# Declaring the two banks of a two-bank PSUM tile independent of each other

## The chip, the core and the metric

The kernel runs on one core of one Trainium2 chip. The metric is the device time of one execution in microseconds. The engines are named as in the profile: PE is TensorE (matrix products), DVE is VectorE, ACT is ScalarE, POOL is GpSimd, SP is SyncE, which issues the DMAs. PSUM is the memory that TensorE writes its products to; it is divided into banks of 512 fp32 numbers per partition.

## The reference

For each of four batches the reference normalises the columns of `q` and `k`, forms a 256 by 256 score matrix, takes its softmax and multiplies `v` by it. The 24,320 rows that result go through a feed-forward layer with a rational activation, 256 to 2048 to 256:

```
qn = q / (norm(q, axis=1) + 1e-6);  kn = k / (norm(k, axis=1) + 1e-6)
s = kn.transpose(0, 2, 1) @ qn / tau        # one 256 x 256 matrix a batch
a = softmax(s)
x = (v @ a).reshape(24320, 256)             # v: (4, 6080, 256)
h = x @ w_in                                # 256 -> 2048
P = a0 + a1*h + a2*h**2 + a3*h**3
Q = 1 + |b0|*|h| + |b1|*h**2
out = (P / (Q + 1e-6)) @ w_out              # 2048 -> 256
```

## The kernel before, in words

**Tiling.** The softmax matrix and `w_in` are multiplied into one fused weight for each batch, so that the main work goes straight from `v` to `h`. The rows are taken in groups of 512 (the twelfth group of a batch has 448), 48 groups in all. The 2048 hidden columns are taken in pairs of two times 128 columns, eight pairs a group, 384 pairs in all. A pair's `h` is a PSUM tile *hx* of two banks, one for each 128 columns. There are three such tiles, six banks; the other two banks are *acc*, into which the group's output is summed.

**One pair** (function `pair`, line 744). The steps that matter here, in the order of their data:

- *mm1(0)* and *mm1(1)* (line 758) on TensorE: six matmuls each, the first six into the low bank of hx, the other six into the high bank.
- Passes over both banks at once, 128 x 1024 elements: ScalarE reads hx for absolute values or squares and for the slope (lines 783 to 804), VectorE forms *prod* in some pairs (line 785) and *num1* (805), and *num2* (807), which writes the numerator without its constant back into hx. The denominator is made in the SBUF tile d, and from it ScalarE makes an approximate reciprocal r, in two passes.
- Operations on one bank each, 128 x 512, once for i = 0 (low bank) and once for i = 1 (high bank), lines 830 to 859. In half of the pairs (kind "S"): GpSimd multiplies d by r, *quot* on VectorE (line 819) multiplies hx by r in place, and *last* (line 825) makes g from d and hx. In the other half (kind "R"): quot writes its result to the SBUF tile gh, GpSimd multiplies d by gh, *rest* on VectorE (line 822) makes d from hx and d, and GpSimd makes gl. So the last reader of a bank is *last* in one half of the pairs and *rest* in the other.
- The second product (line 771) on TensorE, from g, or from gh and gl, into acc.

**Other users of hx tiles.** The score products of the next batch go to the low bank alone (line 541 and following); the transposed exponentials (line 668) and the fused weights (line 681) go to the high bank alone; the transposed rows of `v` (line 718) use both banks.

**What sets the order.** The kernel doesn't issue its steps as they are written. Each step is handed to a planner (class `Planner`, line 113) with an engine, a cost, a key (a due time) and the buffers that it reads and writes. The planner simulates the five engines and gives out one order of steps for each; `order()` is at line 159. To the planner the two banks of an hx tile are two buffers, "hA" and "hB", with users of their own: mm1(0) of a new pair may be placed as soon as the old pair's last user of hA is through, although hB of the same tile is still in use, and mm1(1) later. Then the steps are issued in that order. The wrapper `InOrder` (line 54) pins every instruction behind the one before it on its engine, so an engine's order is the planner's.

**What sets the waits.** The waits between engines are not the planner's. The framework that the kernel is written in follows every access to a tile and puts a semaphore wait wherever it finds that one instruction depends on an earlier one of another engine. The hx tiles are allocated whole, two banks in one tile.

Of the kernel before, what the change touches and what calls it, by code (L numbers as in the profile page):

```python
# [20 lines left out]
LAG = {  # L21
    "first": (-23.943, 0.779, 16.152, -2.628, 12.275, -14.299, 0.849, 12.204),
    "second": (64.578, 55.323, 59.143, 56.607, 7.413, 49.338, 52.686, 69.362),
    "line": (11.809, -44.33, -0.798, -23.493, 7.232, -28.691, -20.654, -32.78),
    "prod": (-25.799, -25.066, -7.177, -0.027, 1.503, -30.754, -29.951, -14.021),
    "abs": (22.851, -16.828, -6.381, 4.349, 3.845, 0.375, -1.748, -5.521),
    "slope": (-2.413, -14.175, 23.292, -11.592, 10.064, 22.358, 14.327, 33.823),
    "num1": (102.929, 82.894, 81.158, 62.614, 64.142, 120.209, 89.073, 104.516),
    "num2": (-4.828, -66.826, -23.076, -34.364, -51.549, -56.374, -41.833, -65.959),
# [24 lines left out]
class InOrder:  # L54


    def __init__(self, tc, engine):
        self.tc, self.engine = tc, engine

    def __getattr__(self, name):  # L60
        op = getattr(self.engine, name)

        def issue(*args, **kwargs):
            ins = op(*args, **kwargs)  # L64
            self.tc.keep_in_program_order(ins)
            return ins

        return issue
# [40 lines left out]
def flat(bufs):  # L109
    return [x for b in bufs for x in (b.both if isinstance(b, Pair) else [b])]  # L110
# [162 lines left out]
def tile_channel_attention_rational_ffn(  # L273
# [12 lines left out]
    nc = tc.nc  # L286
# [22 lines left out]

    FRONT = 12  # L310

    pe = InOrder(tc, nc.tensor)
    dve = InOrder(tc, nc.vector)
    act = InOrder(tc, nc.scalar)
    pool = InOrder(tc, nc.gpsimd)
    sp = InOrder(tc, nc.sync)

    SLOTS = {"hA": 3, "hB": 3, "acc": 1, "d": 3, "uu": 4, "r": 3, "gh": 6, "gl": 4, "g": 4, "w": 9, "kq": 4, "sq": 2, "ssq": 1,
# [27 lines left out]
    def banks(view=None):  # L346


        def whole(slot):
            t = homes["hx"][slot].rearrange("p (a b) -> p a b", a=2)  # L350
            return t if view is None else view(t)

        return Pair(Buf("hA", whole), Buf("hB", whole))

    def bank(tag):
        return Buf(tag, lambda slot: homes["hx"][slot][:, 512 * (tag == "hB") :][:, :512])

    def step(eng, cost, key, fn, reads=(), writes=(), port=False, rank=None):
        new = [b for b in flat(writes) if b.tag is not None and not b.writers]

        def run():
            for b in new:
                b.tile = b.view(b.slot)
            fn()

        plan.add(eng, cost, key, run, reads, writes, port, rank)

# [126 lines left out]
    class Attn:  # L494
# [3 lines left out]
        def __init__(self, b, begin, pace, end, gate=()):  # L498
            self.b, self.gate, self.kq = b, gate, [None, None]
            self.ssq = None  # L500
            first = b == 0
            sps = bank("hA") if first else None
            self.sacc = None if first else buf("sacc", [P, 512], F32)
            self.front = FRONT if b == 1 else 0
            if self.front:
                sps = buf("acc", [P, 2 * GT], F32, "fronts")
            for i in range(2 * NG):
                if i < self.front:
                    at = both = TIME["front"] + i * TIME["front_pace"]
                else:  # L510
                    at, both = begin + i * pace, begin + (i if first else i + 1 - i % 2) * pace
                self.half(i, at, both, sps)
            self.scores = sps if first else self.sacc
            self.softmax(end)
# [229 lines left out]
    def pair(m, at, vparts, w, acc):  # L744
        G, p = divmod(m, NFP)
        pn = groups[G % NG][1]
        n = T * pn
        s = n / 512
        (vhi, vlo), (whi, wlo) = vparts, w
        hx = banks()  # L750
        d, r = buf("d", [P, 2, GT]), buf("r", [P, 2, GT])
# [27 lines left out]
        def cost(per, fixed):  # L779
            return per * s + fixed  # L780

        if kind[1] == "F":
            fn = lambda: act.activation(c(kk), c(hx), AF.Abs, scale=b1)
            step("ACT", cost(0.87, 0.25), at + LAG["first"][p], fn, [hx], [kk], rank=at + 1.0)
            fn = lambda: dve.scalar_tensor_tensor(c(d), c(kk), b0, c(hx), op0=ALU.add, op1=ALU.mult)
            step("DVE", cost(1.06, 0.22), at + LAG["prod"][p], fn, [kk, hx], [d], rank=at + 1.0)
            fn = lambda: act.activation(c(d), c(d), AF.Abs)
            step("ACT", cost(0.87, 0.17), at + LAG["abs"][p], fn, [d], [d])
        else:
            fn = lambda: act.activation(c(d), c(hx), AF.Square)  # L790
            step("ACT", cost(0.87, 0.16), at + LAG["first"][p], fn, [hx], [d], rank=at + 1.0)
            fn = lambda: act.activation(c(kk), c(hx), AF.Abs, scale=b0)
            step("ACT", cost(0.87, 0.25), at + LAG["second"][p], fn, [hx], [kk], rank=at + 1.0)
            if kind[1] == "A":
                fn = lambda: act.activation(c(d), c(d), AF.Identity, scale=b1, bias=ONE)
                step("ACT", cost(0.87, 0.27), at + LAG["line"][p], fn, [d], [d])
            else:
                fn = lambda: pool.tensor_scalar(c(d), c(d), b1, ONE, op0=ALU.mult, op1=ALU.add)
                step("POOL", cost(1.06, 0.07), at + LAG["line"][p], fn, [d], [d])
            fn = lambda: pool.tensor_tensor(c(d), c(d), c(kk), op=ALU.add)  # L800
            step("POOL", cost(2.32, 0.06), at + LAG["sum"][p], fn, [d, kk], [d])

        fn = lambda: act.activation(c(y), c(hx), AF.Identity, scale=a3, bias=a2)
        step("ACT", cost(0.87, 0.33), at + LAG["slope"][p], fn, [hx], [y], rank=at + 3.0)
        fn = lambda: dve.tensor_tensor(c(y), c(y), c(hx), op=ALU.mult)
        step("DVE", cost(1.06, 0.16), at + LAG["num1"][p], fn, [y, hx], [y])
        fn = lambda: dve.scalar_tensor_tensor(c(hx), c(y), a1, c(hx), op0=ALU.add, op1=ALU.mult)
# [3 lines left out]
        fn = lambda: act.activation(c(r), c(d), AF.Abs_reciprocal_sqrt, bias=more)  # L811
        step("ACT", cost(0.87, 0.2), at + LAG["root"][p], fn, [d], [r], rank=at + 6.0)
        if kind[1] == "F":
            fn = lambda: pool.tensor_scalar(c(d), c(d), ones[:, 0:1], ONE, op0=ALU.mult, op1=ALU.add)
            step("POOL", cost(1.06, 0.07), at + LAG["one"][p], fn, [d], [d])
        fn = lambda: act.activation(c(r), c(r), AF.Square)
        step("ACT", cost(0.87, 0.2), at + LAG["square"][p], fn, [r], [r])

        def quot(i, out):
            dve.scalar_tensor_tensor(out, hx[:, i, :n], a0, r[:, i, :n], op0=ALU.add, op1=ALU.mult)  # L820

        def rest(i, out):
            dve.scalar_tensor_tensor(out, hx[:, i, :n], a0, d[:, i, :n], op0=ALU.add, op1=ALU.subtract)

        def last(i, out):
            dve.scalar_tensor_tensor(
                out, d[:, i, :n], 2.0, hx[:, i, :n], op0=ALU.subtract, op1=ALU.mult, reverse0=True
            )

        for i in range(2):  # L830
            h, key = hx.both[i], at + 0.1 * i
            old = [acc] if p or i else []
            end = p == NFP - 1 and i == 1
            t = Buf()
            if kind[0] == "S":
                g = buf("g", [P, GT])
                fn = lambda i=i: pool.tensor_tensor(d[:, i, :n], d[:, i, :n], r[:, i, :n], op=ALU.mult)
                step("POOL", cost(1.16, 0.06), key + LAG["again"][p], fn, [d, r], [t])
                step("DVE", cost(0.53, 0.23), key + LAG["quot"][p], lambda i=i: quot(i, hx[:, i, :n]), [h, r], [h])
                step("DVE", cost(0.53, 0.16), key + LAG["last"][p], lambda i=i, g=g: last(i, g[:, :n]), [d, t, h], [g], rank=at + 10.0)  # L840
                fn = lambda i=i, g=g, end=end, old=old: mm2(i, (w_out_sb,), (g,), not old, end)
                step("PE", 1.72 * s, key + LAG["out"][p], fn, [g, w_out_ok[p], *old], [acc])
                continue
            ghi, glo = buf("gh", [P, GT], F32R), buf("gl", [P, GT], F32R)
            step("DVE", cost(0.53, 0.2), key + LAG["quot"][p], lambda i=i, g=ghi: quot(i, g[:, :n]), [h, r], [ghi], rank=at + 10.0)
            fn = lambda i=i, g=ghi: pool.tensor_tensor(d[:, i, :n], d[:, i, :n], g[:, :n].bitcast(F32), op=ALU.mult)
            step("POOL", cost(1.16, 0.06), key + LAG["again"][p], fn, [d, ghi], [t])
            if kind[2] == "D":
                step("DVE", cost(0.53, 0.23), key + LAG["rest"][p], lambda i=i: rest(i, hx[:, i, :n]), [h, d, t], [h])
                fn = lambda i=i, g=glo: dve.tensor_tensor(g[:, :n], hx[:, i, :n], r[:, i, :n], op=ALU.mult)  # L850
                step("DVE", cost(0.53, 0.16), key + LAG["last"][p], fn, [h, r], [glo], rank=at + 10.0)
            else:
                left = Buf()
                step("DVE", cost(0.53, 0.2), key + LAG["rest"][p], lambda i=i: rest(i, d[:, i, :n]), [h, d, t], [left])
                fn = lambda i=i, g=glo: pool.tensor_tensor(g[:, :n], d[:, i, :n], r[:, i, :n], op=ALU.mult)
                step("POOL", cost(1.16, 0.06), key + LAG["last_pool"][p], fn, [d, left, r], [glo], rank=at + 10.0)
            fn = lambda i=i, g=ghi, old=old: mm2(i, (w_out_hi, w_out_lo), (g, g), not old, False)
            step("PE", 0.92 * s, key + LAG["out"][p], fn, [ghi, w_out_ok[p], *old], [acc])
            fn = lambda i=i, g=glo, end=end: mm2(i, (w_out_hi,), (g,), False, end)
            step("PE", 0.46 * s, key + LAG["out_lo"][p], fn, [glo, w_out_ok[p], acc], [acc])  # L860
# [37 lines left out]
    for G in range(TG):  # L898
        b, g = divmod(G, NG)
        at = T0 + G * NFP * II  # L900
# [47 lines left out]
```

## Time and profile before

| | |
|---|---|
| median of 3 runs | 2874.55 us (2873.23 to 2874.65) |
| the profiled execution | 2872.88 us |
| its span, first to last instruction | 2871.1 us |
| TensorE matmuls busy | 2642.3 us (92% of the span) |
| VectorE busy | 2480.3 us (86%) |
| ScalarE busy | 2246.2 us (78%) |
| GpSimd busy | 2290.1 us (80%) |

How to read the profile: busy time is the union of an engine's instructions. In rows of operations, `hx<-vhi,w` means that the tile hx is written from vhi and w; buffer numbers are left out, and 128x512 is partitions by elements. All instructions carry line 64, that of the wrapper, so they are told apart by their tiles: `d<-hx,coef,d` is rest, `g<-d,hx` is last, `hx<-hx,coef,r` and `gh<-hx,coef,r` are quot, `hx<-uu,coef,hx` is num2, `hx<-vhi,w` and `hx<-vlo,w` are mm1. `PE hx L64 <- DVE d L64: 84.0, 96, 1.6` in the view of waits says that TensorE, before instructions that write hx, was idle for 84.0 us in 96 places, at most 1.6 us in one, until a VectorE instruction that writes d had ended.

### The profile page before, as it was taken

Reading aid. Unit: us, or ns where it says so; the run is one execution under the profiler, and the core shown is the slowest. Engines: PE = TensorE matmul, PEld = TensorE weight load, DVE = VectorE, ACT = ScalarE, POOL = GpSimd, SP = SyncE. Lnnn points to the kernel's source line nnn. Section 1 sums busy time; section 2 is a strip of 40 time slices with the busy share of each in tenths; the row PEclk is TensorE's granted clock in tenths of the full one; section 3 lists DMA queues with packets and bytes.
Section 4 is the critical chain, followed back from the end, with each engine's and each line's share of the span. In section 5 each row is a group of like instructions: output and inputs, shape, how many; then the busy total and the mean of one; then the engine's idle time right before and its main releaser. Section 6 shows DMA issues by size and latency. Waiting matters only on the chain.

```text
span 2871.1 us, 30342 instructions
## 1 busy us (share of the span) xinstructions
PE 2642.3 (92%) x10304; PEld 1858.2 (65%) x10304; DVE 2480.3 (86%) x2911; ACT 2246.2 (78%) x2285; POOL 2290.1 (80%) x1725
## 2 busy tenths in 40 slices
PE   7899999999998999999999999999999999999998
PEld 6666667666665666666676666666677666666666
DVE  8888898898978989987788998898788898898897
ACT  5777787687778878877778888787787888788886
POOL 6697788787768878878977888788896788787786
PEclk9999999999999999999999999999999999999999
DMA  8300002000100000002210000001220000000000
GB/s 306 125 15 15 30 8 79 15 15 29 41 18 15 23 22 15 22 29 81 74 57 14 30 15 15 30 15 45 73 72 23 22 15 15 30 15 15 29 8 14
DMA packets 69324, 109.97 MB, mean 38 GB/s; under 512 B 5296, under 2 KB 53936, under 8 KB 69168
## 3 DMA queue, kind: packets, MB, share of 16 engines
q1 hardware_dynamic: 69168, 108.03, 11.2%
q8 instruction: 81, 1.33, 0.2%
q14 instruction: 75, 0.61, 0.1%
HBM read 83.10 MB, written 24.90 MB: 38 GB/s over the span
## 4 chain that ended last, share of the span: by engine, by line
PE 48%; DVE 33%; issue 6%; POOL 6%; ACT 5%; DMA 0%; DVEq 0%; SPq 0%; POOLq 0%; ACTq 0%
PE hx L64 31%; PE acc L64 17%; DVE hx L64 12%; DVE d L64 7%; DVE uu L64 6%; DVE g L64 5%; POOL d L64 4%; DVE gh L64 3%; ACT uu L64 2%; ACT r L64 1%; ACT d L64 1%; POOL gl L64 1%; POOL ssq L64 1%; POOL orow L64 1%; ACT sq L64 0%
## 5 line engine op out<-in xcount | busy, mean ns | idle before, releaser
L64 PE MATMUL hx<-vhi,w 128*128 128x512 f32 (+1 forms) x3072 | 1097.3, 411 | 181.7 <-DVE d L64 77.8
L64 PEld LDWEIGHTS hx<-vhi,w 128*128 128x128 f32 x3072 | 578.5, 188 | 450.3 <-DVE d L64 136.5
L64 POOL TENSOR_TENSOR d<-d,gh 128x512 f32<-128x512 f32 (+1 forms) x384 | 484.1, 1281 | 267.4 <-DVE gh L64 266.9
L64 PE MATMUL acc<-g,w_out_sb 128*128 128x512 f32 (+1 forms) x1536 | 688.9, 587 | 1.1 <-DVE g L64 1.1
L64 ACT ACTIVATE uu<-hx,babs 128x1024 f32<-128x1024 f32 (+1 forms) x384 | 423.8, 1104 | 276.7 <-PE hx L64 276.7
L64 PE MATMUL hx<-vlo,w 128*128 128x512 f32 (+1 forms) x1536 | 600.5, 391 | 0.0
L64 POOL TENSOR_TENSOR gl<-d,r 128x512 fp32r<-128x512 f32 (+1 forms) x384 | 489.3, 1281 | 74.5 <-DVE d L64 70.9
L64 POOL TENSOR_TENSOR d<-d,r 128x512 f32<-128x512 f32 (+1 forms) x384 | 480.8, 1273 | 39.4 <-ACT r L64 36.5
L64 DVE SCALAR_TENSOR_TENSOR hx<-uu,coef,hx 128x1024 f32<-128x1024 f32 (+1 forms) x384 | 488.8, 1273 | 3.5
L64 DVE TENSOR_TENSOR uu<-uu,hx 128x1024 f32<-128x1024 f32 (+1 forms) x384 | 461.5, 1202 | 29.9 <-ACT uu L64 29.9
L64 PEld LDWEIGHTS acc<-g,w_out_sb 128*128 128x128 f32 x1536 | 289.9, 189 | 273.2 <-issue 254.9
L64 ACT ACTIVATE uu<-hx,coef 128x1024 f32<-128x1024 f32 (+1 forms) x384 | 457.3, 1191 | 0.0
L64 ACT ACTIVATE d<-d 128x1024 f32<-128x1024 f32 (+1 forms) x288 | 301.0, 1045 | 170.6 <-DVE d L64 165.6
L64 ACT ACTIVATE r<-d 128x1024 f32<-128x1024 f32 (+1 forms) x384 | 401.6, 1047 | 39.9 <-POOL d L64 37.0
L64 ACT ACTIVATE r<-r 128x1024 f32<-128x1024 f32 (+1 forms) x384 | 402.1, 1048 | 5.8
L64 DVE SCALAR_TENSOR_TENSOR d<-uu,babs,hx 128x1024 f32<-128x1024 f32 (+1 forms) x288 | 364.1, 1264 | 45.8 <-ACT uu L64 42.3
L64 POOL TENSOR_SCALAR d<-d,ones 128x1024 f32<-128x1024 f32 (+1 forms) x288 | 321.9, 1118 | 86.3 <-ACT r L64 86.1
L64 DVE SCALAR_TENSOR_TENSOR d<-hx,coef,d 128x512 f32<-128x512 f32 (+1 forms) x384 | 282.7, 741 | 123.8 <-PE hx L64 79.5
L64 DVE SCALAR_TENSOR_TENSOR g<-d,hx 128x512 f32<-128x512 f32 (+1 forms) x384 | 256.9, 679 | 99.8 <-PE hx L64 78.4
L64 PEld LDWEIGHTS hx<-vlo,w 128*128 128x128 f32 x1536 | 290.1, 189 | 58.5 <-issue 13.8
L64 DVE SCALAR_TENSOR_TENSOR hx<-hx,coef,r 128x512 f32<-128x512 f32 (+1 forms) x384 | 288.2, 751 | 22.6 <-ACT r L64 12.9
L64 DVE SCALAR_TENSOR_TENSOR gh<-hx,coef,r 128x512 fp32r<-128x512 f32 (+1 forms) x384 | 269.3, 740 | 25.3 <-ACT r L64 15.0
(101 smaller groups left out, 2982.5 us busy)
## 6 DMA issues: line engine op xcount, KB each, us to landing
vst<-in_v_dram SPq DMA_DIRECT2D x44, 512.0 KB, 3.4
out_dram<-orow SPq DMA_DIRECT2D x44, 512.0 KB, 2.6
kq<-in_k_dram SPq DMA_DIRECT2D x78, 256.0 KB, 3.4
kq<-in_q_dram SPq DMA_DIRECT2D x78, 256.0 KB, 3.7
d<-in_moe_w_in_dram SPq DMA_DIRECT2D x8, 512.0 KB, 6.5
r<-in_k_dram SPq DMA_DIRECT2D x10, 256.0 KB, 6.0
r<-in_q_dram SPq DMA_DIRECT2D x10, 256.0 KB, 6.0
d<-in_moe_w_out_dram SPq DMA_DIRECT2D x4, 512.0 KB, 5.6
```

The costliest lines, as they stand in the source:

```text
L64: ins = op(*args, **kwargs)
```

## The change

The steps, their instructions and the order stay. Each step that uses a single bank of an hx tile, and is either a step of TensorE or one of those marked `lone` (quot, rest and last of a pair), now notes which slot and bank it uses while its instructions are issued. For every instruction of such a step, the new function `apart` goes through the last 40 noted instructions on the other bank of the same tile and tells the framework, for those of another engine, that the two don't depend on each other. Steps over both banks and steps of ScalarE note nothing; neither do VectorE's steps for the score sums and the fused weights.

```
     half = [None]
     seen = {}

     def apart(eng, ins):
         if half[0] is None:
             return
         slot, bank = half[0]
         for other, old in seen.get((slot, 1 - bank), ()):
             if other is not eng:
                 tc.declare_no_dep(ins.ins, old.ins, reason="the two use different banks of one tile")
         mine = seen.setdefault((slot, bank), [])
         mine.append((eng, ins))
         del mine[:-40]
```

`InOrder` calls it after each instruction, and `step` sets the note:

```
-    def step(eng, cost, key, fn, reads=(), writes=(), port=False, rank=None):
+    def step(eng, cost, key, fn, reads=(), writes=(), port=False, rank=None, lone=False):
         new = [b for b in flat(writes) if b.tag is not None and not b.writers]
+        own = {id(b): b for b in (*flat(reads), *flat(writes)) if b.tag in ("hA", "hB")}
 
         def run():
             for b in new:
                 b.tile = b.view(b.slot)
+            used = {(b.slot, b.tag == "hB") for b in own.values()}
+            half[0] = used.pop() if len(used) == 1 and (eng == "PE" or lone) else None
             fn()
+            half[0] = None
...
-                step("DVE", cost(0.53, 0.23), key + LAG["quot"][p], lambda i=i: quot(i, hx[:, i, :n]), [h, r], [h])
+                step("DVE", cost(0.53, 0.23), key + LAG["quot"][p], lambda i=i: quot(i, hx[:, i, :n]), [h, r], [h], lone=True)
```

The other steps of quot, rest and last get `lone=True` in the same way.

More of the change, by code (lines that the diff above doesn't have):

```diff
@@ L54, with __init__ @@
 class InOrder:
-    def __init__(self, tc, engine):
-        self.tc, self.engine = tc, engine
+    def __init__(self, tc, engine, log=None):
+        self.tc, self.engine, self.log = tc, engine, log
     def __getattr__(self, name):
@@ L65, in issue @@
             self.tc.keep_in_program_order(ins)
+            if self.log is not None:
+                self.log(self, ins)
             return ins
@@ L310, in tile_channel_attention_rational_ffn @@
     FRONT = 12
[L312 to L315, printed above, removed]
+    half = [None]
+    seen = {}
+    def apart(eng, ins):
+        if half[0] is None:
+            return
+        slot, bank = half[0]
[5 more added lines that the diff above has]
+        del mine[:-40]
+    pe = InOrder(tc, nc.tensor, apart)
+    dve = InOrder(tc, nc.vector, apart)
+    act = InOrder(tc, nc.scalar, apart)
+    pool = InOrder(tc, nc.gpsimd, apart)
     sp = InOrder(tc, nc.sync)
@@ L838, in pair @@
                 step("POOL", cost(1.16, 0.06), key + LAG["again"][p], fn, [d, r], [t])
-                step("DVE", cost(0.53, 0.23), key + LAG["quot"][p], lambda i=i: quot(i, hx[:, i, :n]), [h, r], [h])
-                step("DVE", cost(0.53, 0.16), key + LAG["last"][p], lambda i=i, g=g: last(i, g[:, :n]), [d, t, h], [g], rank=at + 10.0)
+                step("DVE", cost(0.53, 0.23), key + LAG["quot"][p], lambda i=i: quot(i, hx[:, i, :n]), [h, r], [h], lone=True)
+                step("DVE", cost(0.53, 0.16), key + LAG["last"][p], lambda i=i, g=g: last(i, g[:, :n]), [d, t, h], [g], rank=at + 10.0, lone=True)
                 fn = lambda i=i, g=g, end=end, old=old: mm2(i, (w_out_sb,), (g,), not old, end)
@@ L844, in pair @@
             ghi, glo = buf("gh", [P, GT], F32R), buf("gl", [P, GT], F32R)
-            step("DVE", cost(0.53, 0.2), key + LAG["quot"][p], lambda i=i, g=ghi: quot(i, g[:, :n]), [h, r], [ghi], rank=at + 10.0)
+            step("DVE", cost(0.53, 0.2), key + LAG["quot"][p], lambda i=i, g=ghi: quot(i, g[:, :n]), [h, r], [ghi], rank=at + 10.0, lone=True)
             fn = lambda i=i, g=ghi: pool.tensor_tensor(d[:, i, :n], d[:, i, :n], g[:, :n].bitcast(F32), op=ALU.mult)
@@ L848, in pair @@
             if kind[2] == "D":
-                step("DVE", cost(0.53, 0.23), key + LAG["rest"][p], lambda i=i: rest(i, hx[:, i, :n]), [h, d, t], [h])
+                step("DVE", cost(0.53, 0.23), key + LAG["rest"][p], lambda i=i: rest(i, hx[:, i, :n]), [h, d, t], [h], lone=True)
                 fn = lambda i=i, g=glo: dve.tensor_tensor(g[:, :n], hx[:, i, :n], r[:, i, :n], op=ALU.mult)
-                step("DVE", cost(0.53, 0.16), key + LAG["last"][p], fn, [h, r], [glo], rank=at + 10.0)
+                step("DVE", cost(0.53, 0.16), key + LAG["last"][p], fn, [h, r], [glo], rank=at + 10.0, lone=True)
             else:
                 left = Buf()
-                step("DVE", cost(0.53, 0.2), key + LAG["rest"][p], lambda i=i: rest(i, d[:, i, :n]), [h, d, t], [left])
+                step("DVE", cost(0.53, 0.2), key + LAG["rest"][p], lambda i=i: rest(i, d[:, i, :n]), [h, d, t], [left], lone=True)
                 fn = lambda i=i, g=glo: pool.tensor_tensor(g[:, :n], d[:, i, :n], r[:, i, :n], op=ALU.mult)
```

## The prediction

> **What bounds the kernel now.** I read the page first (busy times, clock, chain), then the windows, then the waits of TensorE and of VectorE from 100 us on, then a timeline of a few microseconds. The page's first part, its clock row and its chain:
>
> ```profile
> span 2871.1 us, 30342 instructions
> ...
> PE 2642.3 (92%) x10304; PEld 1858.2 (65%) x10304; DVE 2480.3 (86%) x2911; ACT 2246.2 (78%) x2285; POOL 2290.1 (80%) x1725
> ...
> PEclk9999999999999999999999999999999999999999
> ...
> PE 48%; DVE 33%; issue 6%; POOL 6%; ACT 5%; DMA 0%; DVEq 0%; SPq 0%; POOLq 0%; ACTq 0%
> ```
>
> No engine is full. TensorE comes nearest, at a clock of 0.9 or more all through, and the chain that ended last passes between TensorE (48%) and VectorE (33%): the two wait for each other. The windows give the stretch between the preparation of the weights and the last group:
>
> ```profile
> core 0: us, PE busy (x) PEld busy (x) DVE busy (x) ACT busy (x) POOL busy (x), PEclk, DMA share, GB/s
> 100.00:2850.00 2750.00, 2552.68 (x9945) 1786.84 (x9945) 2386.99 (x2766) 2184.57 (x2205) 2225.95 (x1689) 1.00 0.09 30
> ```
>
> Of these 2750 us TensorE is idle for 2750.0 - 2552.7 = 197.3 and VectorE for 2750.0 - 2387.0 = 363.0. DMA has a share of 0.09 and bounds nothing. The waits say what ended that idle time (total, times, longest):
>
> ```profile
> PE hx L64 <- DVE d L64: 84.0, 96, 1.6
> PE hx L64 <- DVE g L64: 74.4, 89, 3.7
> PE hx L64 <- DVE hx L64: 17.1, 36, 1.7
> ...
> DVE d L64 <- PE hx L64: 79.5, 67, 4.2
> DVE g L64 <- PE hx L64: 78.4, 71, 1.8
> DVE d L64 <- ACT uu L64: 42.3, 52, 3.2
> DVE d L64 <- POOL d L64: 37.9, 41, 2.7
> DVE uu L64 <- ACT uu L64: 29.9, 18, 3.6
> DVE gh L64 <- ACT r L64: 15.0, 8, 3.2
> DVE hx L64 <- ACT r L64: 12.9, 31, 0.9
> ```
>
> TensorE waited 84.0 + 74.4 + 17.1 = 175.5 us, 89% of its 197.3, for VectorE before a matmul into an hx tile. VectorE waited 79.5 + 78.4 = 157.9 us, in 67 + 71 = 138 stalls, for TensorE's matmuls into hx. The second sum is the odd one. The VectorE operations that stall there are *rest* (d<-hx,coef,d) and *last* (g<-d,hx). What they read in hx was rewritten by VectorE itself in *num2*, a whole pass after the pair's own matmuls; their other input comes from GpSimd. No matmul makes any data for them. The wait can only be for matmuls of the next pair, which have begun in the other bank of the same tile. The timeline shows one such knot (start, length, idle before and who ended it):
>
> ```profile
> 1731.37 1.14 POOL L64 TENSOR_SCALAR d<-d,babs 128x1024 f32<-128x1024 f32 x1
> 1731.60 0.68 DVE L64 SCALAR_TENSOR_TENSOR g<-d,hx 128x512 f32<-128x512 f32 x1
> ...
> 1732.22 0.62 PE L64 MATMUL acc<-gh,w_out_lo 128*128 128x512 f32 x2
> 1732.32 0.76 DVE L64 SCALAR_TENSOR_TENSOR hx<-hx,coef,r 128x512 f32<-128x512 f32 x1
> ...
> 1733.13 0.50 PE L64 MATMUL hx<-vhi,w 128*128 128x512 f32 x1 [0.29 <-DVE hx L64]
> ...
> 1734.42 0.39 PE L64 MATMUL hx<-vhi,w 128*128 128x512 f32 x1
> 1734.90 0.69 DVE L64 SCALAR_TENSOR_TENSOR g<-d,hx 128x512 f32<-128x512 f32 x1 [1.83 <-PE hx L64]
> ...
> 1735.65 0.50 PE L64 MATMUL hx<-vhi,w 128*128 128x512 f32 x1 [0.84 <-DVE g L64]
> ```
>
> *last* of the low bank ends at 1732.28 and frees it. TensorE is through with acc at 1732.84 and could begin the next pair there, but waits 0.29 us for *quot* on the high bank (hx<-hx,coef,r). Then *last* of the high bank, whose hx input is ready at 1733.08, waits 1.83 us until the sixth matmul into the low bank has ended. Because it is that late, TensorE's second block, into the high bank, waits 0.84 us; this wait is for a true use of the bank, but its length is the false wait's doing.
>
> **The change, part by part.** It adds no instruction and no wait and leaves each engine's order; the bookkeeping runs while the program is built. It takes out waits between TensorE steps that use one bank and VectorE's quot, rest and last, where the two use different banks of one tile.
>
> VectorE's false waits. By the argument above all 138 stalls of rest and last on TensorE fall away: 157.9 us of VectorE's time.
>
> TensorE's false waits. Those ended by quot (17.1 us) are all false, since last or rest on the same bank still follows and it is that which frees the bank. Those ended by rest and last (84.0 + 74.4) are of three sorts: false, as the first block's in the knot can be; true but made long by a stall of VectorE, as the 0.84 us; or true without one. The view doesn't part them. As 138 stalls of VectorE face 96 + 89 = 185 of these waits, most belong to the first two sorts. TensorE's side is therefore worth between 17.1 and 175.5 us. It can be worth a little more, because a record outlasts the pace:
>
> ```profile
> 1734.18 0.40 PE L64 MATMUL hx<-vlo,w 128*128 128x512 f32 x1
> ```
>
> It takes 0.40 us, but the next matmul starts 0.24 later (the row at 1734.42). So 0.16 us of each of the 96 + 89 + 36 = 221 stalls is counted as busy, an estimate of 35 us, and the ceiling is 175.5 + 35 = 210 us. The Trainium skill, "Perfetto Trace Analysis", Identifying the Most-Contended Engine, goes further: matmul busy time says little of the room left, and the weight loads' share is to be read. By that TensorE (65%) would have far more room than VectorE (86%), and a floor would be VectorE's 2480 us. The trace agrees with the first half, by the 0.16 us; for the second no run here shows room beyond the waits, and the sum does without it.
>
> How the two add up. They don't: in the knot the same 1.8 us stands in both ledgers. A microsecond is gained only if both engines gain it, so I take the smaller, VectorE's 157.9. From it goes what comes late next. When rest and last come early, VectorE meets its next operation's inputs from ScalarE and GpSimd early too, and its waits for these, 42.3 + 37.9 + 29.9 + 15.0 + 12.9 = 138.0 us now, grow. The trace doesn't show by how much. One bound is today's density, 138.0 us on 2387.0 of work, which makes 158 x 0.058 = 9 us; the other is all 157.9. I take 26, a sixth, nearer to the low end, because the nearest row is the knot: GpSimd is already at its next operation at 1731.37, so the input of the stalled *last* had lain ready about 3.5 us when it ran. The gain is 157.9 - 26 = 132 us.
>
> The other pairs that become independent (score products, transposes of the exponentials, fused weights, each in one bank) are costed at nothing: what they wait for is mostly the true owner of their bank, and waits on quot, rest and last stand in the rows above already.
>
> The profiled execution took 2872.9 us, 1.8 more than its span; the sum against it is 2872.9 - 132 = 2741 us. The median of the runs, 2874.55, lies 0.06% above it, which I neglect. About 0.2% (6 us) is what a measurement of this kernel can tell from no change.
>
> **The rivals.** (a) *The gain is handed back.* VectorE runs early into ScalarE and GpSimd, which are 78% and 80% busy and partly fed by TensorE, and waits there instead. For it: 138.0 us of such waits exist. Against: both engines have some 20% of slack, and GpSimd in the knot was ahead. If two thirds of 157.9 return, the gain is 53 us: 2820.
>
> (b) *The change doesn't do what it says.* Each instruction waits until an engine's count of finished work reaches a value. Where the operation truly needed stands behind the falsely needed one in that order, the wait stays the same. For it: the second block's wait in the knot is of that kind. Against: rest and last need nothing of TensorE at all, so there no other operation can keep the wait. If nothing moves: 2873.
>
> (c) *Slower.* While TensorE writes one bank, VectorE now reads and writes its neighbour in the same tile, which the old waits forbade. Should the 138 freed operations be held up by it, they would take longer. These are the rows (min/median/max, ns; the last is an operation of this size that was held up, in the preparation of the weights):
>
> ```profile
> L64 DVE SCALAR_TENSOR_TENSOR d<-hx,coef,d x384: 673/746/752, 117.2 to 2855.8; 128x512 f32<-128x512 f32 x176, 128x448 f32<-128x448 f32 x16
> L64 DVE SCALAR_TENSOR_TENSOR g<-d,hx x384: 609/683/690, 129.4 to 2861.0; 128x512 f32<-128x512 f32 x176, 128x448 f32<-128x448 f32 x16
> ...
> L64 DVE SCALAR_TENSOR_TENSOR d<-uu,d x6: 672/688/1895, 76.3 to 96.9; 128x512 uint32<-128x512 uint32 x4, 128x512 f32<-128x512 f32 x2
> ```
>
> The held-up one took 1.895 - 0.688 = 1.2 us more. At that price 138 operations cost 166 us against 157.9 gained: 2881 us. It decides from 157.9 / 138 = 1.14 us an operation. Against: with TensorE busy 92% of the time and writing other tiles, the slowest of 384 is 7 ns from the median. The Trainium skill, "PSUM — Partial Sum Buffer", PSUM bank collisions, puts the conflict at the single bank and says that accesses to different banks run clean; by that the price is nothing. The rows agree for banks of other tiles, and for the two banks of one tile no run here shows it yet.
>
> (d) *More than forecast:* the ceiling of TensorE's side, 210 us, with nothing returned: 2663.
>
> **How the numbers follow.** The forecast, a gain of 60 to 210 us, has 0.80. Handed back, 6 to 60 us, has 0.11. Nothing moves 0.05, slower 0.03, beyond the ceiling 0.01. The range runs from the ceiling, 2663, to about where two thirds are handed back, 2825. Faster by over 0.2% is 0.80 + 0.11 + 0.01 = 0.92; within it 0.05; slower 0.03.
>
> **What would show it.** In the profile after, "DVE d <- PE hx" and "DVE g <- PE hx" should nearly vanish and "PE hx <- DVE hx" with them; "PE hx <- DVE d" and "<- DVE g" should fall together from 158 to 60 or less. VectorE's waits for ScalarE and GpSimd should rise by some 26 us; if they rise by 100, it is rival (a). Counts and durations should stay: medians of 746 ns for rest and 683 for last; were they to grow by tenths of a microsecond, it is (c). TensorE's busy share of the span should rise to about 95%. The prediction is wrong if the time falls by less than 48 us, or if it falls while those rows of VectorE on TensorE stay.

## The result, and the profile after

The changed kernel takes 2692.7 us in the median (2692.11 to 2693.56, 4 runs), the kernel before 2874.18 beside it. The ratio is 0.937, with a 95% interval of 0.935 to 0.939: 181.5 us or 6.3% faster. The forecast was 2741 us, with a range of 2663 to 2825. The gain is larger than the 132 us that the sum gave.

The page of the changed kernel, the lines that answer to those of before:

```profile
span 2691.8 us, 30390 instructions
...
PE 2601.5 (97%) x10304; PEld 1864.0 (69%) x10304; DVE 2473.1 (92%) x2911; ACT 2238.9 (83%) x2285; POOL 2287.1 (85%) x1725
...
DVE 38%; PE 33%; POOL 11%; issue 8%; ACT 8%; DMA 1%; SPq 0%; DVEq 0%; POOLq 0%; ACTq 0%
```

Each engine executes as many operations as before. The 48 instructions more are of the kind that isn't counted as busy. The profiled span is 2871.1 - 2691.8 = 179.3 us shorter. TensorE's busy time became shorter by 2642.3 - 2601.5 = 40.8 us, VectorE's by 2480.3 - 2473.1 = 7.2. For each of the two the rest of the 179.3 is idle time that went. In the chain that ended last, TensorE's share fell from 48% to 33%; VectorE's rose from 33% to 38% and GpSimd's from 6% to 11%.

The waits of TensorE and VectorE from 100 us on (total, times, longest), in the order of the rows of before:

```profile
PE hx L64 <- DVE d L64: 6.3, 21, 1.6
PE hx L64 <- DVE g L64: 26.2, 24, 2.0
...
DVE d L64 <- ACT uu L64: 25.9, 23, 3.2
DVE d L64 <- POOL d L64: 54.0, 65, 2.8
DVE uu L64 <- ACT uu L64: 27.0, 19, 3.2
DVE gh L64 <- ACT r L64: 15.4, 10, 3.2
DVE hx L64 <- ACT r L64: 13.4, 28, 1.7
```

Three rows are gone altogether: VectorE's rest and last on TensorE (157.9 us before) and TensorE on quot (17.1). TensorE's other waits for VectorE at hx fell from 158.4 to 6.3 + 26.2 = 32.5 us. VectorE's waits for ScalarE and GpSimd were 138.0 us and are 25.9 + 54.0 + 27.0 + 15.4 + 13.4 = 135.7: in sum, what VectorE gained didn't come back there. The sum hides two movements: GpSimd's row rose by 54.0 - 37.9 = 16.1 us, and ScalarE's four fell from 100.1 to 81.7, by 18.4. The knot of the prediction, at the same pair, in the timeline of the changed kernel:

```profile
1628.11 0.69 DVE L64 SCALAR_TENSOR_TENSOR g<-d,hx 128x512 f32<-128x512 f32 x1
...
1628.83 0.76 DVE L64 SCALAR_TENSOR_TENSOR hx<-hx,coef,r 128x512 f32<-128x512 f32 x1
...
1629.19 0.39 PE L64 MATMUL hx<-vhi,w 128*128 128x512 f32 x1
...
1629.70 0.69 DVE L64 SCALAR_TENSOR_TENSOR g<-d,hx 128x512 f32<-128x512 f32 x1
...
1630.33 0.61 PE L64 MATMUL hx<-vhi,w 128*128 128x512 f32 x2
```

The first matmul into the low bank (1629.19) starts while quot works on the high bank (1628.83 to 1629.59), and *last* of the high bank starts at 1629.70, 0.11 us behind quot, while those matmuls run; before, it stood 1.83 us. The 0.61 us row at 1630.33 holds the sixth matmul into the low bank and the first into the high bank, one right behind the other: the 0.84 us of TensorE are gone too.

The operations themselves didn't become slower (min/median/max in ns, the rows that rival (c) hung on):

```profile
L64 DVE SCALAR_TENSOR_TENSOR d<-hx,coef,d x384: 671/747/754, 118.1 to 2676.5; 128x512 f32<-128x512 f32 x176, 128x448 f32<-128x448 f32 x16
L64 DVE SCALAR_TENSOR_TENSOR g<-d,hx x384: 610/682/691, 130.4 to 2681.7; 128x512 f32<-128x512 f32 x176, 128x448 f32<-128x448 f32 x16
```

### The profile page after: what moved, and what is told of

It is laid out like the page before. It is cut to its first block, busy times and chain, and to the rows that moved or that the text cites. A ratio compares the mean times of both kernels' runs of the same rounds, so it can differ in the third digit from the quotient of the medians.

```text
span 2691.8 us, 30390 instructions
## 1 busy us (share of the span) xinstructions
PE 2601.5 (97%) x10304; PEld 1864.0 (69%) x10304; DVE 2473.1 (92%) x2911; ACT 2238.9 (83%) x2285; POOL 2287.1 (85%) x1725
## 4 chain that ended last, share of the span: by engine, by line
DVE 38%; PE 33%; POOL 11%; issue 8%; ACT 8%; DMA 1%; SPq 0%; DVEq 0%; POOLq 0%; ACTq 0%
PE hx L64 18%; PE acc L64 15%; DVE hx L64 13%; DVE d L64 9%; DVE uu L64 7%; POOL d L64 7%; DVE g L64 4%; DVE gh L64 3%; ACT uu L64 3%; ACT r L64 2%; POOL gl L64 2%; POOL ssq L64 2%; DVE vlo L64 1%; ACT d L64 1%; POOL orow L64 1%
## 5 line engine op out<-in xcount | busy, mean ns | idle before, releaser
L64 DVE SCALAR_TENSOR_TENSOR d<-uu,babs,hx 128x1024 f32<-128x1024 f32 (+1 forms) x288 | 364.2, 1264 | 29.3 <-ACT uu L64 25.9
L64 DVE SCALAR_TENSOR_TENSOR hx<-hx,coef,r 128x512 f32<-128x512 f32 (+1 forms) x384 | 288.4, 751 | 22.7 <-ACT r L64 13.4
L64 DVE SCALAR_TENSOR_TENSOR gh<-hx,coef,r 128x512 fp32r<-128x512 f32 (+1 forms) x384 | 269.4, 740 | 23.9 <-ACT r L64 15.4
```

## The experiments

Theory A is that of the prediction: VectorE's false stall is the root of the knot, and TensorE's second block inherits its length. Rival B says that TensorE's side alone costs. Later runs ask what sets the end now, and whether more waits of this kind can go.

**One direction at a time.** `apart` declares only for instructions of one engine:

```
-            if other is not eng:
+            if other is not eng and eng is dve:      # the other run: eng is pe
```

> Half of the change: only VectorE's rest, last and quot are declared independent of earlier TensorE instructions on the other bank; TensorE still waits for VectorE's operations on the other bank. Theory A (the knot: VectorE's false stall is the root, and TensorE's second block only inherits its length) expects most of the gain here: VectorE's waits on TensorE at rest and last go from 157.9 us to under 5, TensorE's waits on VectorE at hx fall from 175.5 to 70-110 us, with quot's 17 still there, and the time is 2735 to 2785 us. Rival B (TensorE's own false waits are what costs, VectorE's stalls are slack): 2830 us or more.

Measured: 2718.0 us (ratio 0.946, 0.944 to 0.947), 156 us faster than before. The waits:

```profile
PE hx L64 <- DVE g L64: 41.2, 49, 1.5
PE hx L64 <- DVE d L64: 15.4, 42, 1.6
PE hx L64 <- DVE hx L64: 10.9, 36, 1.7
```

VectorE's false stalls are gone, and TensorE's waits at hx fell from 175.5 to 41.2 + 15.4 + 10.9 = 67.5 us, although nothing was declared for TensorE: 108 of the 175.5 were inherited. Even quot's false waits are shorter (10.9 us instead of 17.1). The gain is larger than A expected. VectorE's five rows for ScalarE and GpSimd, however, grew here, from 138.0 to 50.2 + 45.4 + 28.1 + 16.4 + 16.0 = 156.1 us. One of them, which was 42.3 us before and is 25.9 with the whole change:

```profile
DVE d L64 <- ACT uu L64: 45.4, 58, 3.2
```

> The other half: only TensorE's one-bank steps are declared independent of earlier VectorE operations on the other bank; VectorE's rest and last still wait for the next pair's matmuls. Theory A expects little: quot's 17.1 us vanish and some of TensorE's first-block waits, but VectorE's 157.9 us at rest and last stay above 130 and the second block still waits for them; time 2800 to 2857 us. Rival B expects most of the 181 us: 2735 us or less. If the two halves together give 181 us, they add; if they give less, each needs the other.

Measured: 2826.55 us (0.983, 0.981 to 0.985), 48 us faster. The knot stays:

```profile
DVE d L64 <- PE hx L64: 73.3, 60, 4.6
DVE g L64 <- PE hx L64: 51.9, 51, 1.6
```

VectorE still stalls 125.2 us, a little less than A expected, and at the same pair as above *last* waits 1.23 us for the sixth matmul. Rival B falls. The two directions give 156 + 48 = 204 us one by one and 181.5 together, so some 22 us stand in both. The figure is rough: three of the four executions of this run took 2825.6 to 2828.1 us at a granted clock of 0.989, the fourth 2816.4 at 0.994, and the kernel before ran at 0.992 or 0.993; by the fourth it would be 32 us. VectorE's five rows for ScalarE and GpSimd fell here, to 42.0 + 28.3 + 28.0 + 15.0 + 12.8 = 126.1 us; the row shown above fell by 14.0, more than the sum:

```profile
DVE d L64 <- ACT uu L64: 28.3, 19, 3.2
```

**Half of the pairs.** `lone=True` stays at quot and last of kind S only, or at quot and rest of kind R only.

> The change for half of the pairs: quot and last of kind S are declared, quot and rest of kind R are not. VectorE's stalls before the change were 78.4 us at last and 79.5 at rest. Theory A (the gain follows VectorE's ledger) expects half of the 181 us, 75 to 110: 2765 to 2800, with the row of last on TensorE under 3 us and that of rest at 60 to 95. Rival: a stall taken away here only comes back at the next knot of the other kind; the row of rest grows beyond 110 and the gain is under 50 us, 2825 or more.

Measured: 2778.51 us (0.967, 0.965 to 0.968), 96 us faster; rest waits 72.9 us for TensorE, last no longer.

> The other half: quot and rest of kind R are declared, quot and last of kind S are not. Theory A: 75 to 110 us again, 2765 to 2800, the row of rest on TensorE under 3 us and that of last at 60 to 95; the two halves together give about the whole. Rival: under 50 us, 2825 or more, with the row of last beyond 110.

Measured: 2785.0 us (0.969, 0.968 to 0.970), 89 us faster; last waits 79.0 us, rest no longer. Both as A expected. The halves give 185 us, the whole 181.5: a stall taken away at one kind of pair doesn't come back at the other.

**Without quot.** The two quot steps lose their `lone=True`:

```
-                step("DVE", ..., lambda i=i: quot(i, hx[:, i, :n]), [h, r], [h], lone=True)
+                step("DVE", ..., lambda i=i: quot(i, hx[:, i, :n]), [h, r], [h])
```

> The whole change except that quot is not declared. The prediction held the waits ended by quot (17.1 us of TensorE's idle time) to be false and part of the gain. Theory A expects that row to come back at 15 to 30 us and the time at 2705 to 2725 us. Rival: quot's waits are covered, because the block behind them would wait for last or rest soon after in any case; then the time stays within 6 us of the changed kernel's 2692.7.

Measured: 2698.76 us (0.939, 0.937 to 0.940). The row is back with 11.1 us in 36 places, but the time is only 6 us above the changed kernel's and the intervals of the ratios overlap. Neither expectation is met clearly: the false waits for quot are real and worth some 6 us at most.

**More than the change.** In `values`, the transposes note the bank of each half (`half[0] = (slot.low.slot, c)` ahead of the inner loop).

> The change and more: the transposes of the rows of v, a step over both banks, note the bank for each half of their instructions, so that the first four no longer wait for the other bank's last user. In the changed kernel's profile TensorE waits 6.3 us at hx for VectorE's d, most of it of this kind. Expected: that row goes to 2 us or less and the time falls by 0 to 6 us, 2687 to 2693; rival: the wait only moves to the fifth transpose, and nothing is gained.

Measured: 2693.13 us (0.937, 0.936 to 0.938), no difference; the row reads 6.2 us instead of 6.3. The rival holds: a wait for the same VectorE operations stays.

ScalarE's and VectorE's steps for the fused weights could not be declared in this way. They write the buffers w, which matmuls into the other bank read, and a declaration takes away every dependency between two instructions, also the one through w. This was left as it is, and no run tests it.

**What sets the end.** TensorE is at 97%, so its work was cut: the second product's matmuls with gl are not issued (`fn = lambda: None` for that step), an estimated 174 us of TensorE's pace.

> The changed kernel without the 768 matmuls acc<-gl,w_out_hi (the low part's second product is left out of the sum; its inputs are still made, and each engine's order is otherwise the same). It takes about 768 x 0.23 = 174 us of TensorE's pace away. Question: what sets the end now, TensorE (97% busy) or VectorE (92%) with its waits for ScalarE and GpSimd. Theory A (TensorE is now the bound in most places): the time falls by 90 us or more, to 2600 or less. Rival C (VectorE with its 136 us of waits for ScalarE and GpSimd is as near, 2473 + 136 + small gaps = about 2640): it falls by 60 us at most, to 2633 or more.

Measured: 2702.02 us (0.940, 0.939 to 0.942), 9 us *slower* than the changed kernel. Theory A of this run (TensorE is the bound) falls by far; the time is on rival C's side, but a rise was in neither. Page and waits:

```profile
PE 2495.2 (92%) x9536; PEld 1710.9 (63%) x9536; DVE 2472.3 (92%) x2911; ACT 2238.7 (83%) x2285; POOL 2286.2 (85%) x1725
```

```profile
PE hx L64 <- DVE g L64: 63.6, 64, 2.5
PE hx L64 <- DVE d L64: 59.2, 99, 1.8
```

TensorE merely waits more: 122.8 us at hx instead of 32.5. Why the time rises by 9 us is open. The granted clock is lower, 0.986 to 0.989 against 0.992 to 0.994, and within this run the time goes with it: 2705.5 us at 0.986, 2698.2 at 0.989, or 2.4 us for a thousandth. By this estimate the 5 thousandths are worth some 12 us, as much as the rise; no run tests it.

> The kernel before without the same 768 matmuls. Theory A (before, the knot of VectorE and TensorE set the end: VectorE stalls until six matmuls are through, whatever TensorE does elsewhere) expects little: 174 us less of TensorE's work give 20 to 70 us, 2805 to 2855, and VectorE's waits on TensorE at rest and last stay above 110 us. Rival B (TensorE's load set the end before, too): 120 us or more, 2755 or less.

Measured: 2871.01 us (0.999, 0.998 to 1.000), 3 us, even less than A expected here. TensorE's waits at hx rose from 175.5 to 133.9 + 118.4 + 26.4 = 278.7 us. The clock was lower here too, 0.981 to 0.984 against 0.991 to 0.993; by the same estimate that hides some 24 us, and the gain at an equal clock would be about 27, as A expected. Either way it is a small part of 174: TensorE's load was not the bound before either. So VectorE's work was cut instead. *num1* is done on the low bank only; its high bank is left out:

```
-        fn = lambda: dve.tensor_tensor(c(y), c(y), c(hx), op=ALU.mult)
+        fn = lambda: dve.tensor_tensor(y[:, 0, :n], y[:, 0, :n], hx[:, 0, :n], op=ALU.mult)
```

> The changed kernel with num1 done on the low bank only: the multiplication of the high bank's slope by h is left out, the number and order of instructions are the same. By the rows of the two widths (1202 ns for 128x1024, about 680 for a VectorE operation of 128x512) this takes 384 x 0.52 = 200 us off VectorE. The runs with less TensorE work gave nothing, which was against the expectation that TensorE is the bound. Theory D (VectorE with its waits for ScalarE and GpSimd sets the end): the time falls by 70 to 130 us, to 2560 to 2625, where TensorE, at a pace of about 2550 plus the start, becomes the next bound. Rival E (no engine sets the end alone; the fixed order with three hx tiles holds all of them): less than 40 us, 2653 or more.

Measured: 2656.28 us (0.924, 0.923 to 0.926). VectorE's busy time fell by 2473.1 - 2291.3 = 181.8 us, the time by 36. Rival E holds, though 36 is close to its limit of 40. VectorE's waits:

```profile
DVE d L64 <- POOL d L64: 91.4, 107, 3.6
DVE d L64 <- ACT uu L64: 76.4, 94, 3.2
DVE hx L64 <- ACT r L64: 36.3, 51, 2.5
DVE uu L64 <- ACT uu L64: 32.2, 32, 3.2
DVE gh L64 <- ACT r L64: 20.7, 16, 3.7
```

These five sum to 257.0 us, 121.3 more than in the changed kernel: here the freed time is handed back to ScalarE and GpSimd, the very thing that didn't happen with the change.

> The changed kernel with both cuts: num1 on the low bank only and without the 768 matmuls of the low part's second product. If TensorE is the next bound behind VectorE (theory D), taking 174 us of it now counts: at least 40 us below the run with less VectorE work alone. Rival E: within 15 us of that run.

Measured: 2642.32 us (0.920, 0.918 to 0.921), 14 us below the run with less VectorE work alone. Rival E again.

> The kernel before with num1 on the low bank only, again 200 us less for VectorE. Theory D with the knot on VectorE's own path: VectorE was the bound before too, only with 158 us of false stalls in its ledger; the time falls by 90 to 180 us, to 2695 to 2785, and the false stalls stay above 110 us. Rival E (the knot of the two engines sets the pace, whoever has less work): less than 50 us, 2825 or more.

Measured: 2822.41 us (0.982, 0.980 to 0.984), 51 us faster than before, far from D's 90 and just beyond E's 50. The false stalls grew from 157.9 to 101.4 + 99.3 = 200.7 us, and the five rows for ScalarE and GpSimd from 138.0 to 65.1 + 54.2 + 32.4 + 28.1 + 19.3 = 199.1: with less work VectorE comes earlier, to the knot and to the other engines, and stands there.

**VectorE's waits for itself.** The condition in `apart` becomes `if other is not eng or eng is dve`, together with the transposes by bank:

> A candidate beyond the change: the transposes of the rows of v note the bank of each half (no gain on their own), and VectorE's instructions are declared independent of VectorE's own earlier ones on the other bank. Where quot on the high bank follows quot on the low bank, a wait for its own engine costs 0.04 us (the start of 1732.32 after an end of 1732.28) to 0.11 us; the program has 72 such waits fewer. Theory D: the few that go are VectorE's time, a gain of 3 to 8 us, 2685 to 2690. Rival: the waits move to the next instruction, no difference.

Measured: 2669.21 us (0.929, 0.927 to 0.930), 23 us faster than the changed kernel, with intervals apart; it beats both kernels. The gain is larger than expected, and of another kind. The same pair as above:

```profile
1613.85 0.68 DVE L64 SCALAR_TENSOR_TENSOR g<-d,hx 128x512 f32<-128x512 f32 x1
...
1614.44 0.75 DVE L64 SCALAR_TENSOR_TENSOR hx<-hx,coef,r 128x512 f32<-128x512 f32 x1
```

Quot starts 0.59 us after *last*, before that has ended (1614.53); in the changed kernel it starts 0.72 after. VectorE's busy time is 2450.4 us, 22.7 less, because operations overlap; its idle time is the same (2668.5 - 2450.4 = 218.1 against 218.7). My count of 72 waits was the wrong one. In the program, 272 waits for the instruction just before, on the other bank, became 2, most of the others turning into waits for an older instruction, which is done by then: 22.7 / 272 = 0.08 us each.

## Why the prediction was right, point by point

*False waits of VectorE, 157.9 us, all fall away.* Right: both rows are gone, and the run with VectorE's direction alone shows that they were the root. *It adds no instruction and no wait* was not quite right: there are 48 instructions more, none of them counted as busy.

*TensorE's waits are partly inherited.* Right: 108 of 175.5 us went when only VectorE's direction was declared. The records' overhang was estimated at 35 us; TensorE's busy time fell by 40.8.

*"They don't add", so the smaller ledger.* The two ledgers do overlap, by some 22 us between the two directions. But as a cap the smaller one was undersized. TensorE's side lost 175.5 - 32.5 = 143.0 us of waits and 40.8 of overhang, 183.8 in all. VectorE's side lost 157.9 us of stalls, 2.3 at the five rows, 7.2 of busy time and, to make up the span's 179.3, 11.9 in smaller rows and gaps that I had not counted.

*26 us come back as waits for ScalarE and GpSimd.* This is the mis-sized term: it measured -2.3 us. As the price of VectorE alone coming early it was near: with VectorE's direction alone the five rows grew by 18.1 us, and GpSimd's row grew by 16.1 with the whole change. The step that failed is that ScalarE was taken to stay where it is: its four rows fell by 18.4. ScalarE had itself been waiting for TensorE's matmuls into hx. Its largest wait, in the kernel before and in the changed kernel:

```profile
ACT uu L64 <- PE hx L64: 276.7, 188, 6.2
```

```profile
ACT uu L64 <- PE hx L64: 163.1, 124, 6.2
```

With VectorE's direction alone this wait is 205.4 us, with TensorE's alone 226.7. It is TensorE's direction that lowers VectorE's waits for ScalarE and GpSimd: alone it took 11.9 us off the five rows, and beside VectorE's direction it took them from 156.1 to 135.7. GpSimd waited less as well:

```profile
POOL d L64 <- DVE gh L64: 266.9, 147, 4.5
```

```profile
POOL d L64 <- DVE gh L64: 191.9, 109, 4.5
```

but VectorE's row for it grew all the same, so at GpSimd part of the gain was handed back as the term had it. The cut of VectorE's work makes VectorE alone lighter, with the knot gone already, and there 121 of 182 us come back. With these two terms, 26 + 2 us that didn't come back and 7 + 12 of VectorE's ledger that weren't counted, 132 becomes the span's 179.

*TensorE comes nearest to being the bound.* Wrong as a reading, though no number of the sum hung on it: an estimated 174 us less of its work changed the time by -3 and +9 us. At an equal clock, by the estimate above, it would have been a gain of some 27 and 3 us. The Trainium skill, "Perfetto Trace Analysis", Identifying the Most-Contended Engine, says that matmul busy time is no measure of the room left, and by its measure, the weight loads' 69%, TensorE had room: here the runs agree. Its rule to improve the engine with the highest occupancy first, here VectorE with 92%, holds only to a fifth: 182 us less work gave 36.

*The rivals.* (b) fell with the rows. (c) fell: medians of 747 and 682 ns against 746 and 683, with the two banks now in use at once. The Trainium skill, "PSUM — Partial Sum Buffer", PSUM bank collisions, says that accesses to different banks run clean; these rows agree. (a) exists in this kernel, but it is less work for VectorE that sets it off; taking the false waits away handed back 16 us at GpSimd's row and nothing in sum. (d) was not reached: 2692.7 us is above its 2663.

*What stays open.* Since neither cut moves the end by much, the end seems to be set by a loop through several engines. That the three hx tiles with the fixed order make this loop is argued, not shown; a fourth tile or another order was not tried.

## What to carry to other kernels

A wait of an engine for one that makes nothing it reads is false, and its price includes the true waits behind it: declaring VectorE's direction alone also took 108 us from TensorE. Before declaring two instructions independent, look at every buffer that the two share, not only at the one in question. A share of 97% is not yet a bound: cut that engine's work and see; and when a stall between two engines goes, ask which of the other engines were waiting for the same knot, and through which engine, before taking anything off for what is late next.

## What the runs showed of the hardware

Two VectorE operations without a wait between them start 0.59 us apart where the first takes 0.68 (1613.85 to 1614.44); with a wait for the first they start 0.72 apart (1628.11 to 1628.83), 0.13 more. The Trainium skill, "VectorE: DVE Perf Modes", The DRAIN you can't avoid, reports a series of copies in which a semaphore after each cost nothing extra, and says beside it that an operation that isn't held (that needn't wait for the one before it to finish) starts earlier. These operations on PSUM go by the second: without the wait the kernel is 23 us faster, and the transposes by bank, the other edit of that run, gave nothing alone.

The granted clock isn't the same in all executions of one kernel, and the time goes with it: 2816.4 us at 0.994 and 2825.6 to 2828.1 at 0.989 in the run with TensorE's direction alone.
